# The last 64 keys of attention outputs as 64x64 matmuls on the quarters of TensorE's array

## Chip, cores and metric

One core of one Trainium2 chip. The metric is the device time of one execution of the program in microseconds. Engines are called as the profile calls them: PE is TensorE's matmul side and PEld its weight loads, DVE is VectorE, ACT is ScalarE, POOL is GpSimd, SP is SyncE.

## The reference

Talking-heads attention in float32, followed by a two-layer MLP with ELU. Batch 4, 12 heads, 448 keys and queries, head size 64; the MLP has 1792 tokens, 768 to 2048 to 768.

```
scores = scale * np.matmul(q, k.transpose(0, 1, 3, 2))
scores = np.einsum('bhij,hg->bgij', scores, w_pre)
attn = softmax of scores over the keys
attn = np.einsum('bhij,hg->bgij', attn, w_post)
out = np.matmul(attn, v)                 # then to tokens x (heads*64)
h = x @ w_in;  g = elu(h);  y = g @ w_out
```

The change is in `np.matmul(attn, v)`, the attention outputs.

## The kernel before, in words

**Tiles and blocks.** The 448 queries of a batch are cut into tiles of ten rows, and tiles into blocks of 10, 12, 12 and 11 tiles (`BLK`), four blocks a batch, 16 in all. A step takes two tiles (the last of an 11-tile block one); there are N = 92 steps, 23 a batch. In a tile the 12 heads and five of its ten rows fill 60 rows of the array, so that the two mixes over heads are matmuls over 60 or 64 rows.

**Stages of one tile.** `qk` makes raw products of queries and keys for a pair of heads; `keep_qk` copies them out (DVE and ACT) and `send` moves them by DMA on SP to the layout of the scores. `scores` (line 243) mixes heads by four 64x64 matmuls of 448 columns, DVE takes the negated maximum of each tile (line 255), ACT the exponential with its sum (257). `norm` makes reciprocals (DVE, 265 and 266) and scales the second mixing matrix with them (POOL, 270). `post` (line 274, matmuls at 281) mixes heads again and turns the tile so that keys lie on partitions: each matmul takes 64 keys, and its 60 columns are 12 heads by five rows. `keep_post` (ACT, 288) copies the result to `ats[n]`. `av` (line 293, matmuls at 302) makes the outputs, and `keep_av` (DVE, 315) copies them out; the last of a block's three units is sent by SP (319).

**Keys.** 448 keys are three and a half chunks of 128 (NJ = 4). Of the last chunk only 64 keys exist. Even tiles have them on partitions 0 to 63 and odd tiles on 64 to 127; the other half of that chunk in `ats` holds zeros, which were put into the banks of `mixed` once, and `v` carries its last 64 keys on both halves. So `av` runs the last chunk as all others, as 128-row matmuls in which half the rows meet zeros.

**Outputs.** A unit (n, u) is block n and two head pairs (w = 0 and 1) of its six. Each of its 16 matmuls has 128 keys on the rows, one head's 64 values as columns, and the block's 100, 110 or 120 query rows streamed; the two heads of a pair go to the two column halves of the array. Both pairs lie beside each other in one bank. In float32 each matmul is two records on PE and two weight loads on PEld.

**Order.** The order is written out by hand: `manual_schedule` keeps the program's order on each engine. The loop over j (line 409) does, in this order: `norm` of step j+1; `scores` of step j+2 (LOOK = 2); the `send` of the last step's qk; the outputs due at j; qk due at j; `post` and `keep_post` of step j; other planned work. `OUT_AT` (line 378) and `RAW_AT` say at which j a unit of outputs or of qk is due. Outputs fall on every other step and qk on those between; at one j a batch (OUT_AT's 22) both fall together. From j = N - 10 on first matmuls of the MLP are put between.

**Banks.** `bank` (line 154) hands out PSUM banks in turn: six in most of the stage (`six`), for scores, qk and outputs. From j = N - 10 on outputs have two (ps2, ps3) of their own.

Of the kernel before, what the change touches and what calls it, by code (L numbers as in the profile page):

```python
# [9 lines left out]
F32 = mybir.dt.float32  # L10
# [9 lines left out]
R = 10  # L20
RH = R * H
HR = R // 2
# [4 lines left out]
NJ = -(-S // CJ)  # L27
# [99 lines left out]
def attention(ctx, tc, qd, kd, vd, wpre, wpost, xd, dec, moe):  # L127
    nc = tc.nc
# [5 lines left out]
    def pool(name, on=ctx, side="left", **kw):  # L134
        return on.enter_context(tc.tile_pool(name=name, side=side, **kw))
# [3 lines left out]
    small = pool("small", bufs=5)  # L139
# [14 lines left out]
    def bank(name, of):  # L154

        turn.append(None)
        p, tag = of[len(turn) % len(of)]
        return p.tile([128, 512], F32, tag=tag, name=name)

    blocks = [(b, i) for b in range(B) for i in range(NB)]  # L160
    NBL = len(blocks)
    count = [BLK[i][1] for _, i in blocks]
    slots = [c + c % 2 for c in count]

    steps = [(n, list(range(t, min(t + 2, count[n])))) for n in range(NBL) for t in range(0, count[n], 2)]
    N = len(steps)
    first = [steps.index((n, [0, 1])) for n in range(NBL)]
    length = [(c + 1) // 2 for c in count]
    k2, q2, ks, qs, ats, vs, xs, xo = {}, {}, {}, {}, {}, {}, {}, {}
# [37 lines left out]
    def qk(n, hp):  # L207
        m = slots[n] * R
        got = [bank("qk", six) for hh in range(2)]
        if n < 2:  # L210
            for hh in range(2):
                part = slice(hh * 64, (hh + 1) * 64)
                nc.tensor.matmul(  # L213
                    got[hh][:m, :S], q2[n][part, hp, :m], k2[0, hp][part], start=True, stop=True)
            return got
        (qh, ql), (kh, kl) = qs[n], ks[blocks[n][0], hp]
        for i, (q, k) in enumerate(((qh, kh), (qh, kl), (ql, kh))):
            for hh in range(2):
                part = slice(hh * 64, (hh + 1) * 64)
                nc.tensor.matmul(  # L220
                    got[hh][:m, :S], q[part, hp, :m], k[part], start=i == 0, stop=i == 2)
        return got

    def keep_qk(n, got, rooms=()):
        m = slots[n] * R
        out = []
        for hh, copy in ((1, nc.vector.tensor_copy), (0, nc.scalar.copy)):
            for hp, ps in got:
                st = rooms.pop() if rooms else stp.tile([120, S], F32, tag="st", name="st")
                copy(st[:m], ps[hh][:m, :S])  # L230
                out.append((2 * hp + hh, st))
        return out

    def send(n, out, t0=0, t1=None, eng=nc.sync):
        t1 = t1 or slots[n]
        raw = raws[n % 2][:, t0:t1, :]
        for h, st in out:
            lo = FRONT + h
            eng.dma_start(out=raw[lo:lo + (R - 1) * H + 1:H], in_=st[t0 * R:t1 * R])

    def scores(n, ts):
        z = small.tile([128, 2], F32, tag="z", name="z")
        got = []
        ps = [bank("s", mixes) for _ in ts]
        for w in range(2):
            for a in range(len(ts)):
                half = slice(a * 64, a * 64 + (64, RH // 2)[a])
                nc.tensor.matmul(  # L250
                    ps[a][w * 64:(w + 1) * 64, :S], wa[half], raws[n % 2][half, ts[0] + w, :],
                    start=True, stop=True)
        for i in range(len(ts)):
            nm = small.tile([128, 1], F32, tag="nm", name="nm", bufs=6)
            nc.vector.tensor_reduce(nm, ps[i][:, :S], op=ALU.max, axis=AX.X, negate=True)  # L255
            p = pp.tile([128, S], F32, tag="p", name="p")
            nc.scalar.activation(  # L257
                p, ps[i][:, :S], AF.Exp, bias=nm, scale=1.0, accum_out=z[:, i:i + 1])
            got.append(p)
        return got, z  # L260

    def norm(got, z):
        k = len(got)
        rz = small.tile([128, 2], F32, tag="rz", name="rz")
        nc.vector.tensor_scalar_add(rz[:, :k], z[:, :k], EPS)
        nc.vector.reciprocal(rz[:, :k], rz[:, :k])  # L266
        out = []
        for i, p in enumerate(got):
            wz = small.tile([128, RH // 2], F32, tag="wz", name="wz", bufs=5)
            nc.gpsimd.tensor_scalar_mul(wz, wb, rz[:, i:i + 1])  # L270
            out.append((p, wz))
        return out

    def post(pairs):
        for i, (p, wz) in enumerate(pairs):
            last = S // 64 - 1
            for j in range(last + 1) if i == 0 else (last, *range(last)):
                c, half = j // 2, slice(64, 128) if j % 2 or i and j == last else slice(64)
                for w in range(2):
                    part = slice(w * 64, (w + 1) * 64)  # L280
                    nc.tensor.matmul(  # L281
                        mixed[w][half, i, c, :], p[part, j * 64:(j + 1) * 64], wz[part], start=True, stop=True)
# [7 lines left out]

    def av(n, hp):
        m = count[n] * R
        w = hp % 2
        if w == 0:
            xo[n, hp // 2] = bank("xo", spare)
        ps = xo[n, hp // 2]
        for c in range(NJ):
            for hh in range(2):  # L300
                g = 2 * hp + hh
                nc.tensor.matmul(  # L302
                    ps[hh * 64:(hh + 1) * 64, w * m:(w + 1) * m].rearrange("p (t r) -> p t r", r=HR),
                    vs[blocks[n][0], hp][:, c, hh * 64:(hh + 1) * 64],
                    ats[n][:, c, :count[n], :, g * HR:(g + 1) * HR].rearrange("p t w r -> p (t w) r"),
                    start=c == 0, stop=c == NJ - 1,
                )

    def keep_av(n, u):
        b, i = blocks[n]  # L310
        m = count[n] * R
        if u == 0:
            x = xp.tile([128, NP * 120], F32, tag="x", name="x")
            xs[n] = x[:, :NP * m].rearrange("p (c m) -> p c m", c=NP)
        nc.vector.tensor_copy(
            xs[n][:, 2 * u:2 * u + 2],
            xo.pop((n, u))[:, :2 * m].rearrange("p (w m) -> p w m", w=2))
        if u == 2:
            nc.sync.dma_start(out=xd[b][i], in_=xs[n])

# [39 lines left out]
    out = [x for hp in range(4) for x in keep_qk(1, [(hp, qk(1, hp))])]  # L360
# [6 lines left out]
    LOOK = 2  # L367
    work, qks, avs = {}, {}, {}
    spare = mixes = six
# [9 lines left out]
    for n in range(1, NBL):  # L379
        b, i = blocks[n]  # L380
# [7 lines left out]
        if i == (0 if b else 2):  # L388
            for hp in range(NP):
                t = at[hp // 2] - bool(b)  # L390
# [4 lines left out]
    for n in range(NBL):  # L395
        b, i = blocks[n]
# [8 lines left out]

    plan(-LOOK, lambda: nc.gpsimd.memset(raws[1][:FRONT], 0.0))
    DENSE = {N - 3: (0, 0), N - 1: (0, 1), N: (1, 0), N + 1: (1, 1), N + 2: (2, 0)}
    sc, nz, ready = {}, {}, []
    for j in range(-LOOK, N + 3):
        if j == N - 10:  # L410
            op_ctx.close()
            moe.begin()
            spare = [(moe.ps[0], f"ps{i}") for i in (2, 3)]
        if j >= N - 10:
            mixes = [(ps_s, "s0"), (ps_s, "s1")] if (N - j) % 2 else [(moe.ps[0], "ps0"), (moe.ps[0], "ps1")]
        if j == N - 2:
            s_ctx.close()
            raw_ctx.close()
            moe.begin_elu()
        if j == N:  # L420
            spare = [(ps_t, f"t{i}") for i in range(2)]
        if j in DENSE and j >= N:
            moe.first(*DENSE[j])
        if j + LOOK - 1 in sc:
            nz[j + LOOK - 1] = norm(*sc.pop(j + LOOK - 1))
        if 0 <= j + LOOK < N:
            sc[j + LOOK] = scores(*steps[j + LOOK])
        for n, out in ready:
            send(n, out)
        for n, u in avs.get(j, ()):  # L430
            for w in range(2):
                av(n, 2 * u + w)
            keep_av(n, u)
        ready = [(n, keep_qk(n, [(hp, qk(n, hp)) for hp in (2 * u, 2 * u + 1)], rooms)) for n, u in qks.get(j, ())]
        if j in nz:
            post(nz.pop(j))
            keep_post(*steps[j])
        if j in DECODE:
            dec.step()
        for f in work.get(j, ()):  # L440
            f()
        if N - 10 <= j < N:
            moe.loads(j - (N - 10))
        if N - 7 <= j < N:
            moe.ahead(j - (N - 7))
        if j in DENSE and j < N:
            moe.first(*DENSE[j])
        if j >= N - 1:
            moe.elu_first(j - N + 1)
# [676 lines left out]
```

## Time and profile before

| | us |
|---|---|
| median of 3 runs | 808.08 |
| lowest, highest | 806.83, 808.41 |
| profiled execution, its own time | 808.53 |
| profiled execution, span from first to last instruction | 806.7 |
| PE busy in the span | 774.4 |
| DVE, ACT, POOL busy | 579.4, 508.9, 409.0 |

Attention takes about the first 350 us, the MLP the rest. How to read it: busy time is an average over stages, so what a change is worth is read from the stage's own rows. The chain of waits is followed back from the last instruction; a piece named for an engine and line is work on the path, "issue" is time in which the engine waited for nothing that the profile shows. Records of PE are pipelined, so their own durations are longer than their distance from each other.

### The profile page before, as it was taken

Reading aid. Unit: us, or ns where it says so; the run is one execution under the profiler, and the core shown is the slowest. Engines: PE = TensorE matmul, PEld = TensorE weight load, DVE = VectorE, ACT = ScalarE, POOL = GpSimd, SP = SyncE. Lnnn points to the kernel's source line nnn. Section 1 sums busy time; section 2 is a strip of 40 time slices with the busy share of each in tenths; the row PEclk is TensorE's granted clock in tenths of the full one; section 3 lists DMA queues with packets and bytes.
Section 4 is the critical chain, followed back from the end, with each engine's and each line's share of the span. In section 5 each row is a group of like instructions: output and inputs, shape, how many; then the busy total and the mean of one; then the engine's idle time right before and its main releaser. Section 6 shows DMA issues by size and latency. Waiting matters only on the chain.

```text
span 806.7 us, 25145 instructions
## 1 busy us (share of the span) xinstructions
PE 774.4 (96%) x10012; PEld 629.0 (78%) x10012; DVE 579.4 (72%) x1080; ACT 508.9 (63%) x1092; POOL 409.0 (51%) x525
## 2 busy tenths in 40 slices
PE   6899999799899999999999999999999999999998
PEld 2456666566566666678989999999999999999997
DVE  3767667677577776567899898676657777788962
ACT  3777778587687778784788783232157566665440
POOL 7666545474356344244688783266438787500000
PEclk9999999999999999999999999999999999999999
DMA  7686668567686686837998889987636768553331
GB/s 223 203 246 183 202 226 257 186 194 209 199 251 213 180 243 198 221 118 236 332 308 269 284 274 315 332 281 261 219 126 204 221 208 269 191 169 106 116 124 58
DMA packets 92913, 174.60 MB, mean 216 GB/s; under 512 B 21788, under 2 KB 59772, under 8 KB 92796
## 3 DMA queue, kind: packets, MB, share of 16 engines
q1 hardware_dynamic: 75366, 113.37, 43.6%
q0 software_dynamic: 16704, 58.47, 23.0%
q8 instruction: 79, 1.29, 0.7%
q10 hardware_dynamic: 726, 1.15, 0.4%
q14 instruction: 38, 0.31, 0.1%
HBM read 94.04 MB, written 39.35 MB: 165 GB/s over the span
## 4 chain that ended last, share of the span: by engine, by line
PE 86%; DMA 4%; issue 4%; ACT 3%; DVE 2%; POOL 1%; ACTq 0%; POOLq 0%; DVEq 0%
PE y L694 14%; PE y L1048 13%; PE h L986 13%; PE h L599 11%; PE mixed L281 10%; PE xo L302 9%; PE s L250 9%; PE qk L220 7%; DMA raw<-st 2%; DMA raw<-room 1%; ACT p L257 1%; DMA s<-c 1%; ACT at L288 1%; DMA k<-in 0%; PE qk L213 0%
## 5 line engine op out<-in xcount | busy, mean ns | idle before, releaser
L255 DVE TENSOR_REDUCE nm<-s 128x1 f32<-128x448 f32 x180 | 103.8, 617 | 63.7 <-PE s L250 63.5
L257 ACT ACTIVATE p<-s,nm 128x448 f32<-128x448 f32 x180 | 112.7, 632 | 49.9 <-DVE nm L255 48.5
L270 POOL TENSOR_SCALAR wz<-wb,rz 128x60 f32<-128x60 f32 x180 | 79.0, 450 | 99.8 <-DVE rz L266 59.2
L288 ACT COPY at<-mixed 128x480 f32<-128x480 f32 (+1 forms) x184 | 93.4, 566 | 35.4 <-PE mixed L281 35.1
L281 PEld LDWEIGHTS mixed<-wz,p 64*64 64x64 f32 x5040 | 84.9, 135 | 38.8 <-issue 27.7
L281 PE MATMUL mixed<-wz,p 64*64 64x60 f32 x5040 | 99.1, 222 | 11.8 <-issue 10.1
L250 PE MATMUL s<-raw,wa 64*64 64x448 f32 (+1 forms) x720 | 95.4, 569 | 10.9 <-DMA raw<-room 5.0
L302 PEld LDWEIGHTS xo<-at,v 128*64 128x64 f32 x1536 | 75.7, 135 | 32.4 <-ACT st L230 20.4
L1048 PE MATMUL y<-part,hi 128*128 128x448 f32 x336 | 96.4, 367 | 0.0
L302 PE MATMUL xo<-at,v 128*64 128x120 f32 (+2 forms) x1536 | 86.5, 263 | 0.2 <-issue 0.2
L515 ACT CAST hi<-lo 128x1024 fp32r<-128x1024 f32 (+1 forms) x49 | 48.0, 979 | 45.9 <-PE y L1048 34.4
L986 PE MATMUL h<-op,hi 128*128 128x448 f32 x264 | 72.3, 367 | 0.0
L599 PE MATMUL h<-xh,lo 128*128 128x448 f32 x192 | 70.3, 366 | 1.9 <-POOL lo L516 1.8
L599 PE MATMUL h<-xh,hi 128*128 128x448 f32 x192 | 70.7, 368 | 0.0
L599 PE MATMUL h<-xl,hi 128*128 128x448 f32 x192 | 70.1, 365 | 0.0
L694 PE MATMUL y<-gl,hi 128*128 128x448 f32 x192 | 69.8, 363 | 0.0
L694 PE MATMUL y<-gh,hi 128*128 128x448 f32 x192 | 69.8, 363 | 0.0
L694 PE MATMUL y<-gh,lo 128*128 128x448 f32 x192 | 69.7, 363 | 0.0
L1048 PEld LDWEIGHTS y<-part,hi 128*128 128x128 f32 x336 | 63.0, 188 | 6.3
L986 PE MATMUL h<-op,lo 128*128 128x448 f32 x240 | 67.3, 367 | 0.0
L1048 PE MATMUL y<-part,lo 128*128 128x448 f32 x168 | 61.8, 368 | 0.0
L516 DVE TENSOR_TENSOR lo<-lo,hi 128x1024 fp32r<-128x1024 f32 x30 | 38.3, 1276 | 24.9 <-ACT hi L515 22.8
(119 smaller groups left out, 1648.8 us busy)
## 6 DMA issues: line engine op xcount, KB each, us to landing
raw<-st SPq DMA_DIRECT2D x140, 210.0 KB
w<-in POOLq DMA_DIRECT2D x48, 512.0 KB, 6.1
lo<-s SPq DMA_DIRECT2D x58, 256.0 KB
s<-c POOLq DMA_DIRECT2D x48, 256.0 KB, 5.7
raw<-st SPq DMA_DIRECT2D x36, 175.0 KB
v<-in POOLq DMA_DIRECT2D x24, 256.0 KB, 6.1
lo<-half SPq DMA_DIRECT2D x16, 384.0 KB
lo<-sum SPq DMA_DIRECT2D x12, 512.0 KB
```

The lines of the kernel that those rows point to most:

```text
L220: nc.tensor.matmul(got[hh][:m, :S], q[part, hp, :m], k[part], start=i == 0, stop=i == 2)
L250: nc.tensor.matmul(ps[a][w * 64:(w + 1) * 64, :S], wa[half], raws[n % 2][half, ts[0] + w, :], start=True, stop=True)
L255: nc.vector.tensor_reduce(nm, ps[i][:, :S], op=ALU.max, axis=AX.X, negate=True)
L257: nc.scalar.activation(p, ps[i][:, :S], AF.Exp, bias=nm, scale=1.0, accum_out=z[:, i:i + 1])
L270: nc.gpsimd.tensor_scalar_mul(wz, wb, rz[:, i:i + 1])
L281: nc.tensor.matmul(mixed[w][half, i, c, :], p[part, j * 64:(j + 1) * 64], wz[part], start=True, stop=True)
L288: nc.scalar.copy(ats[n][:, :, ts[0]:ts[0] + len(ts), w, :], mixed[w][:, :len(ts)].rearrange("p t c n -> p c t n"))
L302: nc.tensor.matmul(ps[hh * 64:(hh + 1) * 64, w * m:(w + 1) * m].rearrange("p (t r) -> p t r", r=HR), vs[blocks[n][0], hp][:, c, hh * 64:(h ...
L599: self.nc.tensor.matmul(h, w[:, ks], x[:, k, :], start=n == 0, stop=n == 3 * NC - 1)
L694: nc.tensor.matmul(y[u], w[:, ks], g[f][:, u, :], start=f == 0 and n == 0, stop=f == NF - 1 and n == 2)
L986: nc.tensor.matmul(y, p[:, ks], x[:, z], start=q < 2 and k == 0 and n == 0, stop=k == KH - 1 and n == 2, skip_group_check=True)
L1048: nc.tensor.matmul(y, w[:, ks], g[:, x], start=begun is None and k == 0 and n == 0, stop=k == FH - 1 and n == 2, skip_group_check=True)
```

## The change

The last chunk's matmuls become 64x64, with the 64 rows that hold keys and only the even or only the odd tiles as columns (every second tile of the block). At one time even tiles of one pair of heads run on the upper row half and odd tiles of the other pair on the lower half, each with its two heads on the two column halves: four matmuls, four quarters. Since the row halves then write at the same time, each pair has a bank of its own. A unit becomes a generator with two stops: a first set of four right after the scores' matmuls (even tiles of pair 0, odd of pair 1); a copy of one column of pair 1's bank on DVE, between the two reductions of the scores; then the twelve 128-row matmuls, pair 0 first, and the second set (even tiles of pair 1, odd of pair 0). `keep_av` copies the two banks one by one. Units that are due when no scores are left (`j + LOOK >= N`) keep the old form (`whole`).

```diff
-    def scores(n, ts):
+    def scores(n, ts, outs):
...
                     ps[a][w * 64:(w + 1) * 64, :S], wa[half], raws[n % 2][half, ts[0] + w, :],
                     start=True, stop=True)
+        for x in outs:
+            next(x)
         for i in range(len(ts)):
             nm = small.tile([128, 1], F32, tag="nm", name="nm", bufs=6)
             nc.vector.tensor_reduce(nm, ps[i][:, :S], op=ALU.max, axis=AX.X, negate=True)
+            for x in outs if i == 0 else ():
+                next(x)
...
-    def av(n, hp):
+    def av(n, u, whole):
         m = count[n] * R
-        w = hp % 2
-        if w == 0:
-            xo[n, hp // 2] = bank("xo", spare)
-        ps = xo[n, hp // 2]
-        for c in range(NJ):
+        ps = [bank("xo", spare) for _ in range(1 if whole else 2)]
+        xo[n, u] = out = [ps[0][:, w * m:(w + 1) * m] if whole else ps[w][:, :m] for w in range(2)]
+
+        def one(w, hh, c, e=None, **kw):
+            hp = 2 * u + w
+            g = 2 * hp + hh
+            part, tiles = (slice(128), slice(None)) if e is None else (slice(e * 64, (e + 1) * 64), slice(e, None, 2))
+            nc.tensor.matmul(
+                out[w][hh * 64:(hh + 1) * 64].rearrange("p (t w r) -> p t w r", w=2, r=HR)[:, tiles],
+                vs[blocks[n][0], hp][part, c, hh * 64:(hh + 1) * 64],
+                ats[n][part, c, :count[n], :, g * HR:(g + 1) * HR][:, tiles],
+                skip_group_check=True, **kw)
+
+        def last(flip, **kw):
             for hh in range(2):
...
+                for e in range(2):
+                    one(e ^ flip, hh, NJ - 1, e, **kw)
+
+        if not whole:
+            last(0, start=True, stop=False)
+            seen = small.tile([128, 1], F32, tag="seen", name="seen", bufs=2)
+            yield
+            nc.vector.tensor_copy(seen, out[1][:, R:R + 1])
+            yield
+        for w in range(2):
+            for c in range(NJ if whole else NJ - 1):
+                for hh in range(2):
+                    one(w, hh, c, start=whole and w == c == 0, stop=whole and c == NJ - 1)
+        if not whole:
+            last(1, start=False, stop=True)
...
-        nc.vector.tensor_copy(
-            xs[n][:, 2 * u:2 * u + 2],
-            xo.pop((n, u))[:, :2 * m].rearrange("p (w m) -> p w m", w=2))
+        for w, out in enumerate(xo.pop((n, u))):
+            nc.vector.tensor_copy(xs[n][:, 2 * u + w], out)
...
         if 0 <= j + LOOK < N:
-            sc[j + LOOK] = scores(*steps[j + LOOK])
+            now = {(n, u): av(n, u, False) for n, u in avs.get(j, ())}
+            open_av.update(now)
+            sc[j + LOOK] = scores(*steps[j + LOOK], list(now.values()))
...
         for n, u in avs.get(j, ()):
-            for w in range(2):
-                av(n, 2 * u + w)
+            for _ in open_av.pop((n, u)) if (n, u) in open_av else av(n, u, j + LOOK >= N):
+                pass
             keep_av(n, u)
```

## Rows read from the trace of the kernel before

**Rows 1.** The page: span, busy time, and the chain that ended last.

```profile
span 806.7 us, 25145 instructions
...
PE 774.4 (96%) x10012; PEld 629.0 (78%) x10012; DVE 579.4 (72%) x1080; ACT 508.9 (63%) x1092; POOL 409.0 (51%) x525
...
PE 86%; DMA 4%; issue 4%; ACT 3%; DVE 2%; POOL 1%; ACTq 0%; POOLq 0%; DVEq 0%
```

**Rows 2.** Busy time by stretch: engines, granted clock, DMA share, GB/s.

```profile
core 0: us, PE busy (x) PEld busy (x) DVE busy (x) ACT busy (x) POOL busy (x), PEclk, DMA share, GB/s
...
120.00:140.00 20.00, 20.00 (x524) 13.67 (x516) 14.82 (x37) 16.79 (x44) 11.23 (x22) 1.00 0.81 254
...
300.00:320.00 20.00, 20.00 (x522) 14.00 (x522) 14.25 (x37) 16.56 (x43) 7.77 (x16) 1.00 0.67 210
```

**Rows 3.** The chain in order of time, 94 to 135 us: start, us, what.

```profile
97.65 1.83 PE xo L302 x29
...
122.84 0.76 PE s L250 x8
123.59 1.69 PE xo L302 x28
125.28 0.97 PE mixed L281 x56
...
127.01 1.41 PE qk L220 x12
...
130.15 1.55 PE xo L302 x27
```

**Rows 4.** The timeline of one unit of outputs, from 84 us on.

```profile
84.17 1.91 PE L302 MATMUL xo<-at,v 128*64 128x120 f32 x32
84.28 1.16 DVE L255 TENSOR_REDUCE nm<-s 128x1 f32<-128x448 f32 x2 [0.34 <-PE s L250]
```

**Rows 5.** Groups by line and shape, 40 to 340 us: busy us, mean ns, idle before.

```profile
L255 DVE TENSOR_REDUCE nm<-s 128x1 f32<-128x448 f32 x163 | 94.0, 617 | 56.5 <-PE s L250 56.3
...
L302 PEld LDWEIGHTS xo<-at,v 128*64 128x64 f32 x1344 | 66.1, 135 | 30.0 <-ACT st L230 20.4 <-ACT at L288 7.8 <-issue 1.7
...
L315 DVE COPY x<-xo 128x240 f32<-128x240 f32 x21 | 8.5, 407 | 12.2 <-PE xo L302 12.0
...
L315 DVE COPY x<-xo 128x200 f32<-128x200 f32 x12 | 4.4, 366 | 5.5 <-PE xo L302 5.5
```

**Rows 6.** The chain in order of time: PE released by another engine.

```profile
349.51 0.44 POOL wz L270
349.96 0.04 issue
350.00 1.08 PE mixed L281 x53
```

**Rows 7.** The timeline at two units: outputs, and DVE's reduction of the same step.

```profile
69.81 1.69 DVE L265 TENSOR_SCALAR rz<-z 128x2 f32<-128x2 f32 x1
70.08 1.90 PE L302 MATMUL xo<-at,v 128*64 128x120 f32 x32
...
71.62 1.14 DVE L255 TENSOR_REDUCE nm<-s 128x1 f32<-128x448 f32 x2
...
347.67 1.89 PE L302 MATMUL xo<-at,v 128*64 128x120 f32 x32
...
349.68 0.60 DVE L255 TENSOR_REDUCE nm<-s 128x1 f32<-128x448 f32 x1
```

**Rows 8.** The chain in order of time: pieces of the stage that are not work on PE.

```profile
141.71 1.05 issue
...
146.74 3.07 issue
...
197.15 9.24 DMA raw<-st
```

**Rows 9.** The page's DMA queues: packets, MB, share of 16 engines.

```profile
q8 instruction: 79, 1.29, 0.7%
```

More of the change, by code (lines that the diff above doesn't have):

```diff
@@ L289, in keep_post @@
                 ats[n][:, :, ts[0]:ts[0] + len(ts), w, :], mixed[w][:, :len(ts)].rearrange("p t c n -> p c t n"))
-    def av(n, hp):
+    def av(n, u, whole):
         m = count[n] * R
-        w = hp % 2
-        if w == 0:
-            xo[n, hp // 2] = bank("xo", spare)
-        ps = xo[n, hp // 2]
-        for c in range(NJ):
-            for hh in range(2):
[L301 to L307, printed above, removed]
+        ps = [bank("xo", spare) for _ in range(1 if whole else 2)]
[10 more added lines that the diff above has]
+        def last(flip, **kw):
+            for hh in range(2):
+                for e in range(2):
[12 more added lines that the diff above has]
+            last(1, start=False, stop=True)
     def keep_av(n, u):
@@ L407, in attention @@
     DENSE = {N - 3: (0, 0), N - 1: (0, 1), N: (1, 0), N + 1: (1, 1), N + 2: (2, 0)}
-    sc, nz, ready = {}, {}, []
+    sc, nz, ready, open_av = {}, {}, [], {}
     for j in range(-LOOK, N + 3):
```

## The prediction

> **What bounds the kernel now.** I read the page first, then the busy time by stretch, then the chain of waits, then single units in the timeline. The page: TensorE is busy for 774 of 806.7 us and the chain that ended last is 86% PE, so a microsecond off TensorE's own work counts, and so does one that TensorE waits [rows 1]. The change sits in the attention stage, about 40 to 350 us. There TensorE is busy throughout at the full granted clock (1.00, the 2.4 GHz level), VectorE for 14.3 to 14.8 of 20 us [rows 2]. The chain in that stage is a repeating pair of steps, all on PE: scores (0.76), outputs of one unit (1.83, 1.69 or 1.55 for 120, 110 or 100 columns), the mix (0.97), and in the other step qk (1.41) in the outputs' place [rows 3]. VectorE's part hangs beside it: today nothing that TensorE does within a step waits for VectorE's work of the same step.
>
> **Units touched.** Of 48 units (16 blocks of queries, three pairs of head pairs each) the last four run when no scores are left and keep the old order. 44 change: 23 with 120 columns, 9 with 110, 12 with 100.
>
> **What goes and comes on TensorE.** A unit has 16 matmuls, each two records of TensorE; two records run side by side on the two column halves, so there are 16 pairs. 1.83, 1.69 and 1.55 us lie 0.14 us apart for ten columns: 8.75 ns for a pair and ten columns, 105 ns for a pair of 120, 96 of 110, 87.5 of 100, and 0.15 us for the changes of shape [rows 3]. The last key tile has four matmuls, four pairs: 0.42, 0.385 and 0.35 us. In their place come eight matmuls of 60 (or 50) columns in two sets of four, 16 records, four on the four quarters at once. The mix is that form: 56 records of 64x60 in 0.97 us are 14 fours of at most 69 ns [rows 3]; the columns alone (60 at 0.875 ns) are 52. I take 60, near the upper end less the mix's share of the shape change, and 51 for 50 columns. Four sets: 0.24, 0.24, 0.20 us. Saved: 0.18, 0.145 and 0.15 us, so 23 x 0.18 + 9 x 0.145 + 12 x 0.15 = 7.2 us, between 5.6 (69 ns) and 8.5 (52 ns). The number of shape changes stays: the first set follows the scores and the last precedes the mix, both 64x64. Only in the three units that share a step with qk is one added, 0.15 at most each.
>
> The 17 ns a record of the mix [rows 3] decides here against a rule. The Trainium skill (TensorEngine Tiling, Instruction Overhead) says that a matmul carries some 60 cycles of overhead, so that one column lasts as long as 60, and that no tiling factor should be taken from a dimension already small. By an estimate from it, 60 cycles at 2.4 GHz for each of 16 records, the sets would cost 0.40 us and a 120-column unit would save 0.02. That is the fourth rival's result by another road.
>
> **The added wait.** After the first set VectorE reads one column of the second pair's bank, between the two reductions of the scores, and the second pair's twelve 128-row records write that bank, so they wait for the read. Behind the first of them stand all the rest of the unit, then the mix or qk and the next scores; ScalarE's and VectorE's copies of these wait too. Call X the time at which the outputs start today. The reduction starts 0.11 after X (84.28 against 84.17), two of them take 1.16, one 0.617, so the second instruction starts 0.54 after the first [rows 4, 5]. The read is not in the trace. Its lower bound is nothing, its upper the 0.41 of today's whole copy; copies of 240 and 200 elements take 407 and 366 ns, which leaves 0.16 for one element, the same operation from the same memory, and I take that [rows 5]. From an engine's end to a TensorE that waits for it 0.04 to 0.05 pass [rows 6]. So TensorE may go on at X + 0.11 + 0.54 + 0.16 + 0.05 = X + 0.86. Without the wait it would get there after two sets (0.12; they follow the scores without a change of shape and so start before X by the part of the 0.15 that lies there today, between nothing and all of it, I take 0.09), the change (0.15) and six pairs (0.63, 0.58, 0.53): X + 0.80 for 120 columns, 0.75 for 110, 0.68 for 100. A restart also has weights to load that were loaded under other work until now (a load is 135 ns [rows 5]; part overlaps, I take 0.05). The wait costs 0.11, 0.16 and 0.23 us: 23 x 0.11 + 9 x 0.16 + 12 x 0.23 = 6.7 us. With a read of nothing this would be near 1, with 0.41 some 17.
>
> **Where VectorE is late.** That holds where VectorE is free when the scores end. In 14 of the 44 units it is not: it still has casts, weight decoding or a reciprocal that waits for ScalarE, and the reduction starts later than X + 0.11. The first is X = 70.08 with the reduction at 71.62, 1.4 late, behind one small VectorE operation of 1.69 us; the last is 347.67 with 349.68, 1.9 late [rows 7]. Over the 14 the lateness adds to 9.3 us. Today it costs nothing, as the mix needs these sums one step later; now each goes to TensorE in full. It does not shrink by itself: in the qk step before such a unit VectorE starts from TensorE's scores, so it is late relative to them. 0.5 of the sum lies in 193 to 206 us, where the chain runs over a DMA of 9.24 us [rows 8], and is not counted: 8.8.
>
> **Small terms.** VectorE gets the read and one copy more, 0.16 + 0.16 a unit; its idle quarter [rows 2] takes these, and without that cover they would be up to 14 us on it. The second bank comes from the rotation of six, ten taken in two steps in place of nine; the bank is last read by the copies of the qk before it. Weight loads already idle 20.4 us until ScalarE's such copies [rows 5], but the chain has no idle piece there [rows 3], so that lies under the scores: 0, and as much as those copies come later where that cover is gone. No DMA, and nothing on SyncE's or GpSimd's queue, is moved. 44 x 16 more TensorE instructions are 704: 79 packets of 1.29 MB are instructions [rows 9], for 20,024 of PE [rows 1] some 253 a packet, three more packets. The chain has "issue" pieces of 1.05 and 3.07 us at 141.71 and 146.74 [rows 8], 5 us apart; two steps issue 344 (172 records and as many loads) in 6.7 us, so a packet lasts 5 us as well; I add 0.4 us for them, 0 to 2. The Trainium skill (Runtime: NRT & Kernel Launch, Instruction fetch mechanics) says that the fetch is hidden behind the issue of instructions; by it the 0.4 is 0, and the 3.07 us speaks against it. Against that, part of the lateness before 146 us may be waited out in these same pieces: 1.5 off.
>
> **Sum.** -7.2 + 6.7 + 8.8 + 0.4 - 1.5 = +7.2 us. The profiled execution took 808.53 (span 806.7, 1.8 around it): 815.7. It stands 0.45 above the median of the three runs, so 815 for the runs.
>
> **Rivals.** First, **faster: the read stays off TensorE's path.** Price: the 7.2 us saved, less up to 3 of lateness, 801 to 806, say 803. It decides where the read ends before the first pair's records do: 0.06 us less on VectorE is enough in the 120-column units. For it: the read stands behind the first reduction alone and twelve records cover it; the waits for instructions and for DMAs on the chain [rows 8] can swallow lateness. Against: the 14 late units would all have to be covered. Second, **nothing to measure:** the wait costs what the sets save and the lateness is mostly swallowed; 808 within 1.6. Third, **worse: VectorE becomes the bound.** In the two busiest steps it is the extra 0.3 us that pushes each reduction back further, and the second tile's exponential with it; 0.3 in half the units is 7 us more, 822. Fourth, **the four quarters don't run at once** (the change doesn't do what it says): if only two of the four did, the 16 records were eight pairs of 52 ns, 0.42 us, as much as they replace, and 7.2 us of the sum are gone: 822. The mix's 17 ns a record [rows 3] speaks against it.
>
> **How the numbers follow.** Forecast 0.55, faster 0.25, nothing 0.10, VectorE bound 0.06, sets not beside each other 0.04. Three runs of this kernel lie 0.2% apart (806.83 to 808.41), so 0.2% is what can be told from no change. Faster: 0.25 and a third of the second rival, 0.28; same 0.08; slower 0.64. The forecast's own range is 809.5 to 820: a read between nothing and 0.3 us, sets of 52 to 69 ns. To hold 8 in 10 the range has to take in part of the faster case: 803 to 820.
>
> **What would show it.** Right: in the unit's chain two sets of 64x64 records right behind the scores, twelve records, then a gap of PE ended by VectorE's copy, some 0.1 to 0.2 us in ordinary units and 0.5 to 2 near 70, 156 and 348 us; mix and qk as before. The sets: 16 records in about 0.24 us. Wrong: no PE idle before the second pair; a read that takes over 0.3 us; sets at over 69 ns; stretches without late units that get shorter by more than 0.1 us a unit.

## The result: slower by 1.2%, and the profile after

The kernel after the change takes 813.98 us (median of 20 runs, 806.88 to 824.43), the kernel before, run beside it, 803.0 us (20 runs, 798.18 to 810.51): a ratio of 1.012, 95% interval 1.0085 to 1.0155, about 9.7 us (6.8 to 12.4). This ratio and those below leave out the runs that lie over 1.5% above the fastest of their kernel, a second, slower state, so they differ a little from the ratio of the two medians. The predicted 815.0 was made against runs of before at 808; those beside the new kernel lie 5 us lower, so the term to compare is the sum, +7.2.

The page of the kernel after, the lines of [rows 1] and [rows 9]:

```profile
span 814.3 us, 25954 instructions
...
PE 770.6 (95%) x10364; PEld 632.1 (78%) x10364; DVE 584.3 (72%) x1172; ACT 510.0 (63%) x1092; POOL 409.8 (50%) x525
...
q8 instruction: 82, 1.34, 0.7%
...
PE 81%; DMA 7%; DVE 6%; issue 3%; ACT 2%; POOL 1%; ACTq 0%; POOLq 0%; DVEq 0%
```

TensorE is busy 4 us less in a span 8 us longer, and VectorE's part of the chain went from 2% to 6%: TensorE now waits. In which stage, the first matmul of the MLP tells. Timeline of the kernel before and of the kernel after, that row in each:

```profile
351.01 0.47 PE L599 MATMUL h<-xh,hi 128*128 128x448 f32 x1
```

```profile
359.95 0.74 PE L621 MATMUL h<-xh,hi 128*128 128x448 f32 x1
```

The scores start within 0.1 us of each other, so 8.9 us between these two profiles arose in the attention stage. The chain in order of time, the kernel after, beside [rows 3]: one unit on time of 120, of 110 and of 100 columns, each with its scores and mix.

```profile
92.04 0.78 PE s L250 x8
92.82 1.91 PE xo L306 x39
94.73 0.82 PE mixed L285 x56
...
129.64 0.76 PE s L250 x8
130.40 1.87 PE xo L306 x33
132.27 0.82 PE mixed L285 x54
...
136.99 0.77 PE xo L306 x18
137.78 1.01 PE xo L306 x20
138.79 0.82 PE mixed L285 x56
```

Outputs and mix must be read together: the last set has the mix's shape, so the change of shape (0.15) moved out of the mix. 120 columns: 1.91 + 0.82 = 2.73, before 1.83 + 0.97 = 2.80. 110: 2.69, before 2.66. 100: 137.78 - 136.99 + 1.01 + 0.82 = 2.62, before 2.52. What the sets save and what the wait costs nearly cancel in units on time.

The late units are another matter. Timeline of the kernel after, an ordinary unit (79 us) and the late one of [rows 7] (70 us), TensorE's outputs, VectorE's operations, and one row each of ScalarE and GpSimd:

```profile
69.96 0.20 ACT L261 ACTIVATION_READ_ACCUMULATOR p<-s,nm 128x1 f32 x1
...
70.25 0.94 PE L250 MATMUL s<-raw,wa 64*64 64x448 f32 x8
...
70.85 1.80 POOL L198 TENSOR_TENSOR ql<-q,qh 128x720 fp32r<-128x720 f32 x1 [1.53 <-DVE qh L197]
...
70.98 1.69 DVE L269 TENSOR_SCALAR rz<-z 128x2 f32<-128x2 f32 x1
71.01 1.07 PE L306 MATMUL xo<-at,v 64*64 64x60 f32 x20
...
72.78 0.60 DVE L257 TENSOR_REDUCE nm<-s 128x1 f32<-128x448 f32 x1
73.30 0.15 DVE L321 COPY seen<-xo 128x1 f32<-128x1 f32 x1
...
73.51 1.13 PE L306 MATMUL xo<-at,v 128*64 128x120 f32 x20 [1.43 <-DVE seen L321]
...
75.27 0.94 PE L250 MATMUL s<-raw,wa 64*64 64x448 f32 x8
...
79.14 1.09 PE L306 MATMUL xo<-at,v 64*64 64x60 f32 x20
79.39 0.62 DVE L257 TENSOR_REDUCE nm<-s 128x1 f32<-128x448 f32 x1 [0.33 <-PE s L250]
79.93 0.15 DVE L321 COPY seen<-xo 128x1 f32<-128x1 f32 x1
```

At 79 the read starts 0.54 after the reduction and takes 0.15. At 70 the addition ahead of the reciprocal takes 1.69 us, where the next one (75.45) takes 0.15; reduction and read come after it, and TensorE stands for 1.43 us between the two pairs. The prediction has reciprocals that wait for ScalarE among the reasons of lateness. This one doesn't: ScalarE's last sum is read out at 70.16, before the addition starts. By the times it is GpSimd that holds it up: the addition ends at 72.67, and GpSimd's subtraction `ql`, 1.80 us long, at 72.65. The same two stand beside each other in all three batches, before the change too (69.81 + 1.69 = 71.50 in [rows 7], GpSimd's from 69.67 to 71.47). No run took the subtraction away, so this is read from the times and not shown by an experiment. The step, from scores to scores, is 75.27 - 70.25 = 5.02 us; before, it was 3.56. TensorE's waits in the stage (40 to 350 us, and in the last line 350 to 360; us in total, times, longest), the kernel after:

```profile
PE xo L306 <- DVE seen L321: 7.3, 10, 1.4
PE s L250 <- DMA raw<-st: 5.5, 3, 2.7
PE mixed L285 <- issue: 4.7, 7, 1.1
...
PE xo L306 <- DVE seen L321: 2.0, 1, 2.0
```

The new wait heads the list. It is not among those of the kernel before, which has 10.1 us of the mix's issue and 1.5 us of the scores' DMA. [Rows 5] by line and shape, 40 to 345 us, have become:

```profile
L257 DVE TENSOR_REDUCE nm<-s 128x1 f32<-128x448 f32 x161 | 95.5, 618 | 51.2 <-PE s L250 49.0 <-PE xo L306 1.9
...
L306 PEld LDWEIGHTS xo<-at,v 128*64 128x64 f32 x1008 | 49.7, 135 | 17.9 <-DVE seen L321 12.3 <-issue 1.3
L306 PE MATMUL xo<-at,v 128*64 128x120 f32 x504 | 34.5, 275 | 4.9 <-DVE seen L321 4.8
...
L321 DVE COPY seen<-xo 128x1 f32<-128x1 f32 x42 | 6.3, 149 | 2.4 <-PE xo L306 2.3
```

The read is one element in 149 ns, and the second pair's 128-row matmuls (twelve records) are what stands idle for it.

### The profile page after: what moved, and what is told of

The parts are those of the page before. It is cut to its first block, busy times and chain, and to the rows that moved or that the text cites. A ratio compares the mean times of both kernels' runs of the same rounds, so it can differ in the third digit from the quotient of the medians.

```text
span 814.3 us, 25954 instructions
## 1 busy us (share of the span) xinstructions
PE 770.6 (95%) x10364; PEld 632.1 (78%) x10364; DVE 584.3 (72%) x1172; ACT 510.0 (63%) x1092; POOL 409.8 (50%) x525
## 4 chain that ended last, share of the span: by engine, by line
PE 81%; DMA 7%; DVE 6%; issue 3%; ACT 2%; POOL 1%; ACTq 0%; POOLq 0%; DVEq 0%
PE y L716 14%; PE h L1008 13%; PE h L621 13%; PE y L1070 13%; PE xo L306 9%; PE mixed L285 8%; PE s L250 7%; PE qk L220 5%; DMA raw<-st 4%; DVE nm L257 2%; DMA q<-in 2%; ACT p L261 1%; DVE st L230 1%; DVE rz L269 1%; DMA raw<-room 1%
## 5 line engine op out<-in xcount | busy, mean ns | idle before, releaser
L257 DVE TENSOR_REDUCE nm<-s 128x1 f32<-128x448 f32 x180 | 106.4, 617 | 59.6 <-PE s L250 57.3
L306 PEld LDWEIGHTS xo<-at,v 128*64 128x64 f32 (+1 forms) x1888 | 84.1, 134 | 51.0 <-issue 16.4
L306 PE MATMUL xo<-at,v 128*64 128x120 f32 (+4 forms) x1888 | 102.1, 254 | 14.2 <-DVE seen L321 9.2
L250 PE MATMUL s<-raw,wa 64*64 64x448 f32 x720 | 92.1, 556 | 15.6 <-DMA q<-in 5.7
L285 PE MATMUL mixed<-wz,p 64*64 64x60 f32 x5040 | 97.1, 221 | 6.1 <-issue 4.7
L89 ACT ACTIVATE sq<-w 128x512 f32<-128x512 f32 x48 | 32.1, 668 | 37.7 <-DVE c L94 37.6
```

Source lines behind the costliest of these rows:

```text
L250: nc.tensor.matmul(ps[a][w * 64:(w + 1) * 64, :S], wa[half], raws[n % 2][half, ts[0] + w, :], start=True, stop=True)
L285: nc.tensor.matmul(mixed[w][half, i, c, :], p[part, j * 64:(j + 1) * 64], wz[part], start=True, stop=True)
L306: nc.tensor.matmul(out[w][hh * 64:(hh + 1) * 64].rearrange("p (t w r) -> p t w r", w=2, r=HR)[:, tiles], vs[blocks[n][0], hp][part, c, hh ...
```

## Experiments

What follows rests on the length of a step, from the start of its scores to the start of the next. Each kind of step comes three times, once in a batch; the shortest of the three is taken as the one freest of waits that come once (at issue, that is for nothing that the profile shows, or for a DMA). Worked out so from the traces of the kernel before (of two profiles, so the shortest of six), the kernel after and four of the experiments, in us. The last row has the three steps above it added as they came, shortest and longest batch:

| step | before | after | wait alone | ScalarE reads | half on quarters | the same, set last |
|---|---|---|---|---|---|---|
| 120 columns, on time | 3.56 | 3.50 | 3.56 | 3.38 | 3.48 | 3.49 |
| 110, on time | 3.42 | 3.44 | 3.41 | 3.26 | 3.36 | 3.37 |
| 100, on time | 3.28 | 3.39 | 3.28 | 3.15 | 3.26 | 3.27 |
| late, 112, 201 and 287 us | 3.53 | 4.03 | 3.91 | 4.00 | 3.63 | 3.47 |
| late, 70, 159 and 245 us | 3.55 | 4.94 | 5.05 | 3.36 | 3.48 | 3.48 |
| the qk step after it | 3.12 | 3.12 | 3.21 | 3.18 | 3.20 | 3.25 |
| the unit after that | 3.74 | 3.69 | 3.75 | 4.00 | 4.09 | 4.10 |
| these three together | 10.65 to 11.50 | 11.77 to 11.86 | 11.97 to 13.30 | 10.79 to 10.96 | 10.77 to 11.12 | 10.98 to 11.25 |

(Times of the kernel after; the others have them some us earlier.) The three rows above the last hang together, and their shortest times don't come from one batch. In the kernel before, where nothing holds TensorE in the late unit (the first two batches of the first profile), the unit two steps behind takes 4.25 and 4.37 us; where a wait at issue of 0.74 to 0.78 us holds it, 3.74 and 3.79. (The prediction and the expectations call such waits at issue waits for instructions; no run shows that.) Timeline of the kernel before, that step in the second batch:

```profile
161.42 0.63 ACT L257 ACTIVATE p<-s,nm 128x448 f32<-128x448 f32 x1
...
161.60 1.56 PE L250 MATMUL s<-raw,wa 64*64 64x448 f32 x8
162.19 0.20 PEld L250 LDWEIGHTS s<-raw,wa 60*64 60x64 f32 x6 [0.43 <-ACT p L257]
```

The scores' weight loads stand for 0.43 us until the exponential has ended, and these scores take 1.56 us where others take 0.94. So VectorE's lateness is not free in the kernel before: some 0.6 us of it come two steps later. A step on time lasts the same in both profiles to 0.02 us.

**The wait without the quarters.** All of the last chunk is done first by 128-row matmuls as before; the two banks, the read and the two copies stay.

```diff
         def last(flip, **kw):
-            for hh in range(2):
-                for e in range(2):
-                    one(e ^ flip, hh, NJ - 1, e, **kw)
+            for w in range(2 if flip == 0 else 0):
+                for hh in range(2):
+                    one(w, hh, NJ - 1, **kw)
```

> The last chunk goes back to four 128-row matmuls, put first in the unit; the read of VectorE, its wait, the two banks and the two copies stay. Theory (the loss is the wait on VectorE's read, above all where VectorE is late): the four matmuls (0.42 us) now also lie ahead of the wait, so that ordinary units do not wait, and units where VectorE is 1.4 us late or more still wait some 1 us: 5 to 8 us slower than the kernel before, and PE idle until the read of 5 to 7 us. Rival (the small matmuls, their instructions or the second bank are the loss): within 2 us of the kernel before.

Measured: 808.61 us (12 runs) against 802.45 (27), ratio 1.008 [1.0048, 1.0111], some 6 us (3.9 to 8.9). The timeline of the late unit of the third batch, VectorE's operations and the outputs behind the wait:

```profile
237.53 1.69 DVE L269 TENSOR_SCALAR rz<-z 128x2 f32<-128x2 f32 x1
...
239.33 0.60 DVE L257 TENSOR_REDUCE nm<-s 128x1 f32<-128x448 f32 x1
239.85 0.15 DVE L321 COPY seen<-xo 128x1 f32<-128x1 f32 x1
...
240.06 0.85 PE L306 MATMUL xo<-at,v 128*64 128x120 f32 x12 [1.13 <-DVE seen L321]
```

The twelve records wait 1.13 us for the read. Units on time are as long as before, to 0.01 us (table), since the last chunk of both pairs and the first pair's twelve records lie ahead of the wait here and cover the read. The late steps at 112, 201 and 287 us grew by 0.4 each, two of those at 70, 159 and 245 us by 1.5 and 1.9, and the stretch from the last unit's scores to the MLP, in which TensorE waits 1.5 us for the read, from 4.29 to 5.44. (In the first batch VectorE was on time at that step, and a wait at issue of 1.14 us made it 4.96; the table takes the other two. In the second batch TensorE stood for 1.27 us at issue, until 153.19, with records next that don't need the read; the read, which ends at 153.20, would have held it as long.) That is 5.7 us, of which, as an estimate from the table, some 1 comes back two steps later, so 4 to 5 of the 6 us. By its rows TensorE waits 3.2 us for the read, where 5 to 7 were expected. So most of this loss stands at the steps where VectorE is late, and it doesn't hang on the quarters.

**The second bank alone.** The kernel before, a bank for each pair and two copies, the matmuls and their order untouched.

```diff
-            xo[n, hp // 2] = bank("xo", spare)
-        ps = xo[n, hp // 2]
+            xo[n, hp // 2] = ([bank("xo", spare) for _ in range(2)], [0, 0]) if two else ([bank("xo", spare)] * 2, [0, m])
+        ps, at = (x[w] for x in xo[n, hp // 2])
...
```

> The kernel before, with a bank for each pair and two copies in place of one, 128-row matmuls as before, no read, no more TensorE instructions. Theory (more instructions): within 2 us of the kernel before. Rival (the second bank shifts the rotation so that TensorE or the copies wait, or the copies delay VectorE): 4 to 8 us slower than before.

Measured: 803.37 us (12 runs) against 803.44 (23), ratio 0.9967 [0.9924, 1.001]. The bank and the copy cost nothing that these runs can tell (6 us faster to 1 slower), as the prediction counted them.

**More instructions alone.** The kernel before, each matmul of the last chunk split into even and odd tiles: 704 TensorE instructions more, the number that the change adds, in one bank and the old order.

```diff
-        for c in range(NJ):
+        for c, e in [(c, None) for c in range(NJ - 1)] + ([(NJ - 1, 0), (NJ - 1, 1)] if split else [(NJ - 1, None)]):
+            tiles = slice(None) if e is None else slice(e, None, 2)
...
```

> The kernel before, with each matmul of the last chunk cut into one for the even and one for the odd tiles, 128 rows, same bank, same order, no read: 16 more TensorE instructions a unit (704 in all), the same columns. Theory (the half-set kernel, which has no wait, lost 8 us against its shorter units through its 704 more instructions, which are fetched by DMA): 5 to 9 us slower than before, of which at most 1.4 are the eight more records' own overhead. Rival (the second bank and copy): within 2 us of the kernel before.

Measured: 805.41 us (12) against 803.44 (23), ratio 1.0028 [0.9996, 1.006]. That instructions in themselves cost 5 to 9 us falls; at most about 5 are left. They aren't free either: its units on time take 3.61, 3.49 and 3.38 us, 0.05, 0.07 and 0.10 more than before, some 3 us over the 44 units, where at most 1.4 was expected.

**The read by ScalarE.** It reads between its two copies of the mix, ahead of any reduction; the second copy is held back until then. Where a unit needs that copy itself (the late kind at 112 us) VectorE still reads.

```diff
-            yield
-            nc.vector.tensor_copy(seen, out[1][:, R:R + 1])
+            on_act = yield
+            (nc.scalar.copy if on_act else nc.vector.tensor_copy)(seen, out[1][:, R:R + 1])
...
-            for x in outs if i == 0 else ():
+            for x in outs if i == 0 and not held else ():
...
-            keep_post(*steps[j])
+            held = keep_post(*steps[j], any(n != steps[j][0] for n, u in avs.get(j + 1, ())) and j + 1 + LOOK < N)
```

> The changed kernel, but the column is read by ScalarE between its two copies of the mix of the step before (the second of them is held back until after the first set); where the unit needs that copy itself, VectorE reads as in the changed kernel. Theory: ScalarE is there about 0.45 us after the scores, the read ends before the first pair's records do, and nearly all of the wait goes: 5 to 7 us faster than the kernel before, 14 to 17 faster than the changed one; PE idle until the read under 3 us. Rival (the small matmuls, their instructions or the second bank are the loss): 3 us or more slower than the kernel before. Other rival (ScalarE's own work is delayed and the exponentials with it): about the kernel before.

Measured: 809.23 us (10 runs), ratio 1.0094 [1.0062, 1.0127]. ScalarE in the timeline, one unit:

```profile
86.91 0.59 ACT L296 COPY at<-mixed 128x480 f32<-128x480 f32 x1
87.39 0.17 ACT L331 COPY seen<-xo 128x1 f32<-128x1 f32 x1
87.45 0.57 ACT L296 COPY at<-mixed 128x480 f32<-128x480 f32 x1
```

The edit does what it should: without a wait the units are 0.18, 0.16 and 0.13 us shorter than before, which is the saving that the prediction priced (0.18, 0.145, 0.15), and the late unit at 70 us is no longer late. The time is missed all the same, and the steps show little of it: the unit at 112 us stays late (+0.47), the last unit waits 1.7 us for ScalarE's read (5.45 us from its scores to the MLP, 4.29 before), and the three steps from the late unit at 70 us on keep the length that they have before where nothing holds TensorE (10.92 and 11.04). TensorE's longest waits that come once, 40 to 350 us, beside those shown of the kernel after:

```profile
PE mixed L289 <- issue: 8.4, 4, 3.8
PE xo L316 <- issue: 3.7, 2, 2.4
PE xo L316 <- DMA v<-in: 1.5, 1, 1.5
```

With the smaller ones they make 15.2 us, and 15.1 and 13.1 in the two profiles of the kernel before, so they don't explain the time either. It stays open.

**The read before both reductions.** VectorE reads first, then reduces.

```diff
         for x in outs:
             next(x)
+            next(x)
...
-            for x in outs if i == 0 else ():
-                next(x)
```

> The changed kernel with VectorE's read ahead of the first reduction of the scores, not behind it. Theory: the wait of ordinary units goes (6.7 us in the prediction), the late units' stays, less 0.54 us each that the reduction took: 2 to 7 us faster than the changed kernel, about the kernel before to 4 us slower. Rival (the wait of ordinary units is the whole loss): 5 us or more faster than the kernel before.

Measured: 809.75 us (6 runs), ratio 1.011 [1.0067, 1.0152]. Some 4 us less than the kernel after by the medians, though the two intervals overlap, and 7 us slower than before, where no loss to a loss of 4 was expected. Units on time become as short as with ScalarE (3.38, 3.26 and 3.16 us), but the late one at 70 us takes 4.48: it is the work ahead of the reduction that is late, and that stands ahead of the read as well.

**Half on the quarters, no wait.** Only the first set is made of 64x64 matmuls; the tiles of the second are 128-row matmuls of half the columns, in which half the rows meet zeros, as before. No read, and nothing of TensorE waits for VectorE.

```diff
-            nc.vector.tensor_copy(seen, out[1][:, R:R + 1])
...
-            last(1, start=False, stop=True)
+            for e in range(2):
+                for hh in range(2):
+                    one(1 - e, hh, NJ - 1, e, full=True, start=False, stop=True)
```

> Only the first set stays on the quarters; the second set's tiles run as 128-row matmuls of half the columns, so that no two row halves meet in a bank and the read and its wait go. Theory: 0.42 us become 0.12 and four pairs of 60 columns at 0.052, 0.09 less in each of 44 units: 3 to 4.5 us faster than the kernel before. Rival (the sets, the instructions or the second bank cost): 2 us or more slower than before.

Measured: 806.84 us (12 runs), ratio 1.0058 [1.0022, 1.0094]: missed, slower by 4 to 5 us where a gain was priced. So the same was run with the set at the unit's end, right before the mix:

```diff
-            last(0, start=True, stop=False)
...
+            last(0, start=False, stop=True)
```

> The half-set kernel (no read, no wait, ratio 1.0058) with its set of four at the end of the unit, in front of the mix, not behind the scores; the same instructions, banks and copies. Theory (the loss comes from work put in front of the unit, where it meets values or banks that are not there yet): 1 to 4 us faster than the kernel before. Rival (the loss comes with the instructions or the two banks, wherever they stand): 3 us or more slower than before.

Measured: 804.19 us (12) against 803.36 (17), ratio 1.0036 [0.9988, 1.0083], from 1 us faster to 7 slower: no gain of the priced size, and no clear difference from before or from the same kernel with its set ahead. Units of both are shorter by 0.07 or 0.08, 0.05 or 0.06 and 0.01 or 0.02 us. In the steps behind the late unit that is taken back. The timeline of the second of the two, around the unit two steps behind the late one (155 us here):

```profile
155.32 1.59 PE L250 MATMUL s<-raw,wa 64*64 64x448 f32 x8
...
155.93 0.20 PEld L250 LDWEIGHTS s<-raw,wa 60*64 60x64 f32 x6 [0.43 <-ACT p L261]
```

It is the wait shown of the kernel before. These two kernels have it behind each of the three late units, the kernel before behind two of three in one profile and none in the other. A shorter unit is not what calls it up: the kernel with more instructions alone, whose units are longer than before, has it behind all three as well (that step takes 4.37 to 4.50 us). The three steps together take 10.77 to 11.25 us here, and 10.92 and 11.04 before where nothing holds TensorE: VectorE and ScalarE set the pace there, and a faster TensorE waits. That is three of a batch's 23 steps. Why the gain of the other units, some 2 us in all, doesn't show in the time, and why the first of the two is 4 to 5 us slower than before, stays open.

**A second look, and shifted instructions.** The kernel before once more as it is, and it and the kernel with ScalarE's read with 32 matmuls of four columns put ahead of everything, so that the packets of instructions end elsewhere.

```diff
...
+    for _ in range(32):
+        nc.tensor.matmul(cold[:120, :4], warm[:, :120], warm[:, :4], start=True, stop=True)
```

> The kernel before, a second profile. Its first profile (808.5) lies 6 us above the median of 27 runs (802.45). Theory (pieces of waiting for instructions and for the scores' DMAs differ from run to run): the steps without such a piece last the same within 20 ns, and the sum of TensorE's idle time, 16.0 us in the first, follows the time. Rival (something else differs): the idle time is the same and the steps differ.

> The kernel before with 32 matmuls of four columns more in the first microseconds, where TensorE waits for data: 128 TensorE instructions, half an instruction packet, so that all packet borders of the attention stage move by half a packet while no step changes. Theory (where packet borders fall among the stage's DMAs decides microseconds, and this is what the kernels without the wait lost): it moves by 2.5 us or more, either way. Rival (borders are a matter of chance in each run and even out): within 2 us of the kernel before.

> The kernel with ScalarE's read (ratio 1.0094) with the same 128 instructions more at the start. Theory (borders): it moves by 2.5 us or more against that kernel. Rival (its loss is in its steps or in its data's DMAs): within 2 us of it, 5 to 9 us slower than the kernel before.

Measured: 805.03 us (one run); 810.88 (6 runs), ratio 1.017 [1.0109, 1.0231]; 826.04 (6), ratio 1.0338 [1.0283, 1.0393]. The last two tell little, because the added matmuls delayed the first step. Timeline of the shifted kernel before, its first scores with what they waited for:

```profile
32.05 3.27 PE L250 MATMUL s<-raw,wa 64*64 64x448 f32 x16 [4.68 <-DMA raw<-room]
```

In the unshifted one they start at 19.20 (second profile; 19.31 in the first). From there to the first matmul of the MLP the shifted kernel takes 1.3 us longer than the second profile of the kernel before and 5.8 less than the first; with ScalarE's read it is 4.3 longer than unshifted. So whether it matters where packets end is not shown either way. The second look says more. The steps without a wait last the same, as expected, but its MLP starts at 343.81, in [rows 1]'s profile at 351.01, and TensorE's waits at issue and for DMAs (13.1 and 15.1 us) make only 2 of these 7 us. Much of the rest are steps behind a long wait: in the first profile a qk step behind a wait of 1.84 us at issue takes 4.74 us (57.48 to 62.22, at a granted clock of 0.64), in the second the same step 3.18, and there are three such steps against one. So what comes once makes 7 us between two profiles of one kernel, and no single profile's total can be read closer.

## Why the prediction was right

**Direction and size.** +7.2 us was predicted and about +9.7 measured, and the mechanism is the one forecast: TensorE waits for the read, a little in units on time, where this takes up what the sets save, and in full in late ones. By kinds of steps, the repeated differences are these. On time, 9 units of 120 at -0.06, 3 of 120 that share a step with qk at +0.08 (4.60 against 4.52 us; the change of shape that the prediction put at up to 0.15 is in it), 6 of 110 at +0.02 and 11 of 100 at +0.11 make +1.0. The late units make +9.1, and 1.8 of that comes back two steps later (both below). That is 8.3 us. One unit at 46 us adds 1.4 once: the casts ahead of its reduction waited for a load of q, and TensorE stood for 1.36 us. That the sum meets 9.7 so closely is chance, as the interval is 6.8 to 12.4. It is chance, too, that the predicted 815 lies 1 us from 813.98: the three runs that it started from, 0.2% apart, lie 5 us above the median of 20, which spread over 1.5%.

**The sets: right.** With the wait out of the way units shrink by 0.18, 0.16 and 0.13 us, so the four quarters do run at once and a 64x60 record costs what it costs in the mix. By an estimate from the 60 cycles of overhead a matmul that the Trainium skill states (TensorEngine Tiling (Array Packing), Instruction Overhead) a 120-column unit would have saved 0.02. This case's trace doesn't agree with the estimate: 3.38 us against 3.56. It puts the overheads of 16 records one behind the other, and a record on four quarters takes 17 ns; how long a record of few columns lasts no run here shows.

**The wait of units on time: right, slightly small.** Between ScalarE's read and the kernel after lie 0.12, 0.18 and 0.24 us a unit (3.38, 3.26 and 3.15 against 3.50, 3.44 and 3.39), where 0.11, 0.16 and 0.23 were worked out. The net with the sets was to be -0.07, +0.015 and +0.08 a unit and is -0.06, +0.02 and +0.11. The read took 0.149 (0.16 was taken), its start 0.54 behind the reduction.

**The late units: right in place, nearly right in size, wrong in one premise.** Those at 70, 159 and 245 us pay 1.4 to 1.5 each, those at 112, 201 and 287 us 0.5 each, and four more 0.09 to 0.24 (the steps from 174, 180, 260 and 267 us). Of the four after 330 us three don't pay: their steps took 3.92, 5.08 and 4.39 us before and 4.04, 5.01 and 4.23 after. The last, the 347.67 of [rows 7], pays most of all. Timeline of the kernel after, and busy time behind the wait:

```profile
356.95 1.58 PE L306 MATMUL xo<-at,v 128*64 128x120 f32 x20 [1.96 <-DVE seen L321]
358.31 1.71 PE L285 MATMUL mixed<-wz,p 64*64 64x60 f32 x56
```

```profile
357.00:361.00 4.00, 4.00 (x79) 3.53 (x80) 1.77 (x6) 1.57 (x6) 1.11 (x3) 0.57 0.02 4
```

TensorE stood for 1.96 us, and behind that the granted clock of the stretch is 0.57, so most of it ran at the 1.2 GHz level; the mix took 1.71 us, 1.08 before [rows 6]. From the last unit's scores to the MLP that is 6.87 us against 4.29. All together 9.1 came, where 8.8 was counted.

The premise that failed is that this lateness costs nothing today. It costs the kernel before some 0.6 us two steps behind each of the units at 70, 159 and 245 us, where nothing holds TensorE (4.25 and 4.37 us; 3.69 to 3.72 after), so 1.8 of the 9.1 are no addition. The 1.5 us taken off is near that by luck, as it stood for another thing, waits at issue that were to absorb lateness. Nor did the 0.4 us for fetching more instructions show: three more packets came (82 for 79), as worked out, but TensorE's idle time at issue did not grow (13.6 us in the first profile of before, 9.7 in the second, 8.8 after, 40 to 350 us).

**The rivals.** VectorE did not become the bound: units and qk steps without lateness keep their length. The faster case's logic, that without the wait the saving arrives, is what the experiments don't bear out. With half on the quarters none of it shows, and in the three steps from the late unit on the exponential's wait takes it back. With the read by ScalarE a saving should be left, as its units on time gain twice as much, and yet it runs 7 us slower than before; with the read before both reductions it is the same. That cause stays open: neither the number of instructions nor the second bank alone makes it, and the waits that come once are no longer in its profile than in those of the kernel before. So the wait is shown as a cost of the kernel after, by its rows and by the kernel that has the wait alone; that it is the only one is not shown, as no kernel that keeps quarters and drops the wait, in whole or in most units, was faster than before. A version with both sets and no read at all wasn't tried, since the read is what orders the two row halves' writes to a bank.

## What to carry to other kernels

A read of one element that lets one engine go on behind another looks free. Here it took 0.12 to 0.24 us from each unit where the reader was on time, as much as the shorter matmuls saved; price it also at the steps where the reader is late, with the full lateness. Slack between two engines is worth keeping: the kernel before let VectorE be 1.4 us late for 0.6 us two steps later. And before making TensorE faster within a step, see which engine is next in that step: here, behind late units, the wait for an exponential took back what shorter matmuls gave.

## What the runs showed that was not expected

The MLP isn't touched, and TensorE is busy all through it, yet its pace differs between profiles. Busy time in a stretch of 100 us, the kernel before in its first profile and, below, in its second:

```profile
500.00:600.00 100.00, 100.00 (x499) 93.39 (x498) 70.21 (x85) 32.63 (x54) 44.76 (x54) 1.00 0.73 244
```

```profile
500.00:600.00 100.00, 100.00 (x486) 90.65 (x486) 60.78 (x79) 31.15 (x53) 41.91 (x53) 1.00 0.67 230
```

499 against 486 records in these 100 us, at a granted clock of 1.00 in both: 13 x 0.2 us = 2.6 us. The profile with the earlier MLP is the slower one in it; the kernel after, whose MLP starts at 359.95, has 499 too. Of the twelve profiles here five have the faster pace and seven the slower, and both occur on one chip, so neither the change nor the chip decides. What makes it was not looked into.

A long wait also costs behind itself. Busy time of the kernel after, the first stretch of [rows 2]:

```profile
120.00:140.00 20.00, 17.28 (x450) 11.91 (x444) 11.67 (x36) 12.97 (x34) 7.87 (x16) 0.91 0.58 177
```

TensorE idled for 2.7 us there, for a DMA of raw products, and the granted clock of the stretch is 0.91: for part of it TensorE ran at the lower level, 1.2 GHz.
